# A hand-ordered attention + gated FFN kernel: TensorE's and ScalarE's steps of five periods in a new order, the other three engines' order kept

## The chip, the cores and the metric

The kernel runs on one core of a Trainium2 chip. The core has TensorE (PE, matrix products; loading a stationary operand is shown as PEld), VectorE (DVE), ScalarE (ACT), GpSimd (POOL) and SyncE (SP), each executing its own list of instructions in order, and 16 DMA engines that move data between the device memory and the on-chip memory. The metric is the device time of one execution in microseconds (us). The time of the kernel before is the median of 3 runs.

## The reference

Two stages follow each other. The first is attention of 64 heads (8 batches × 8 heads, 576 positions, 64 channels per head), in two forms that are added: a coarse one on queries, keys and values averaged over groups of 4 positions (144 by 144), whose result is repeated 4 times, and a local one in which position i sees only the positions j with |i − j| < 4. The second is a gated feed-forward layer on all 4608 positions.

```python
q_d = q.reshape(B, H, Sd, factor, D).mean(axis=3)      # and k_d, v_d; factor = 4
out_d = sm_attn(q_d, k_d, v_d)
out_up = np.repeat(out_d, factor, axis=2)
mask = np.abs(pos[:, None] - pos[None, :]) < factor
scores = np.where(mask, scale * np.matmul(q, k.transpose(0, 1, 3, 2)), -1e9)
out_local = np.matmul(softmax(scores), v)
attn_out = out_up + out_local                            # (8, 8, 576, 64)

x = attn_out.transpose(0, 2, 1, 3).reshape(4608, 512)
gate = np.maximum(x @ w_gate, 0.0)                       # w_gate, w_val: 512 x 1536
val = x @ w_val
return (gate * val) @ w_out                              # w_out: 1536 x 512
```

## The kernel before, in words

Inputs are float32 in memory and are made float16 on the way in; sums are float32 in PSUM, the accumulator memory of TensorE, which has 8 banks of 512 float32 columns.

**Tiling.** The 64 heads are taken as 32 pairs, four pairs to a batch. For the feed-forward layer the 4608 positions are cut into 9 chunks of 512 columns of `xT`, the transposed x. While one chunk goes through the feed-forward layer, the attention of later pairs is worked in between. What follows the start is therefore organised in periods: period c works on chunk c's gate and value products, on the output products of chunk c − 1, and on four head pairs further on (two in each half of the period; the half is the number u in a step's name, the pair of the half its letter a or b).

**The multiplication scheme.** The gate products (x times w_gate) from chunk 2 on and the output products are not done block by block but by a scheme of seven products instead of eight: the operands are cut in 2 × 2 blocks, sums and differences of blocks are formed ahead (VectorE), seven products are formed on TensorE, and the four result blocks come out of sums of products. Here this is class `Half7` (L1250 to L1274). Product 1 is accumulated in a quarter `a` of two PSUM banks; ScalarE copies it to quarter `d` (copy 1); products 6 and 7 are added to it, after copy 2 to quarter `b`, and so on. At the end ScalarE casts two of the result blocks (`finish` 11 and 21, L1270), and VectorE adds for the other two (`finish` 12 and 22, L1272) the saved product 5, which ScalarE had copied out (copy 5). Product 4 is added into the same quarter `a` in which product 7 ended, so TensorE may start it only after `finish` 22 has read that quarter, and `finish` 21 reads it after product 4. A quarter that is read late holds up the next product that goes there.

**The order.** Nothing is planned by a compiler here. A string `SEQ` (L18) holds 2,330 step names; the program runs through it (L1551) and issues each step's instructions to the engines concerned, in this order. Each engine then executes its own instructions in the order in which they were issued, and waits at an instruction until what it reads has been written and what it overwrites has been read. So the place of a name in the string matters only against other names that use the same engine.

**The names.** `kind/argument/u@c` is a step of half u of period c. Those that matter here:

- `sq/j.bank.tile.i`: product i of the gate scheme for blocks j (TensorE, L1254; two matmuls of 256 columns); `sk/….i`: its copy i (ScalarE, L1265); `sf/….11` and `.21`: ScalarE's casts (L1270); `sf/….12` and `.22`: VectorE's additions (L1272).
- `up`, `uk`, `uf`: the same for the output products of the chunk before (six matmuls each).
- `vh/jj.bank`: a value product (TensorE, L910; four matmuls of 512 columns); `gt`: VectorE multiplies it with the gate (L1349).
- `hg`, `hv`, `relu`, `gate`: chunk 1's gate and value products, in the plain way (L910, L919, L922).
- `scores`, `o/…`: attention's matmuls (L807, L811; L838, L853, L858); `exp` (ScalarE, L820) and `ed` (L825): its exponentials; `mask` (VectorE, L833); `ln`, `inv` (ScalarE), `xn`, `xsum` (VectorE): its normalisation.
- `kk/…` (ScalarE, L770): key columns copied into the block-diagonal form that the local scores use; `kd/…` (ScalarE, L777): the same for the pooled keys, after VectorE's pooling `pool` (L530); `zero/…`: one-time clearing.
- `next`, `sum`, `sumhi`, `xq` (VectorE, L989, L1241): operand sums of the seven-product schemes.
- `v1` (L575), `v2` (L567), `tm` (L1483), `tn` (L1424), and the loads `qk`, `v` (L462, L480): GpSimd; `v4`, and some of the transposes (`flip`): SyncE's queue.
- `t:…`: the steps of the last chunks, behind period 6 (L1158 and others).

In the string before, periods 2 to 6 repeat one and the same order. In period 5 (and in each of the others) ScalarE's part of the first half reads: `kk/b0 uk/2.1 sk/4.0.0.1 kk/b1 sf/4.0.0.11 sk/4.0.0.2 sk/4.0.0.5 exp/a0 ed/a kk/a1 sf/4.0.0.21 uk/2.2 uk/2.5 sk/0.0.2.5 …`, and TensorE's: `… sq/4.0.0.6 vh/4.7 sq/4.0.0.3 sq/4.0.0.7 up/2.5 sq/4.0.0.4 up/2.6 sq/0.0.2.1 …`.

Of the kernel before, what the change touches and what calls it, by code (L numbers as in the profile page):

```python
# [48 lines left out]
o/a00/0@1 o/a01/0@1 qk/a3/0@1 zs/1.0/0@1 tn/1/0@1 gate/0/0@1 c21//0@1 o/a10/0@1 ln/a/0@1 p/3/0@1 flip/11 next/3/0@1  # L49
qk/b3/0@1 c12//0@1 relu/2/0@1 qk/b1/0@1 o/a11/0@1 inv/a/0@1 pool/b/0@1 xn/a/0@1 hg/1/0@1 relu/1/0@1 zero/b/1 v2/a/1@1  # L50
hg/4/0@1 zero/b/5 hv/1/0@1 gate/1/0@1 hv/2/0@1 qk/b0/0@1 vd/9/7 vc/9/7 hg/3/0@1 relu/3/0@1 flip/12 gate/2/0@1
xsum/a/0@1 zs/2.0/0@1 scores/b/0@1 exp/b0/0@1 mask/b0/0@1 exp/b1/0@1 mask/b1/0@1 qk/a3/1@1 hv/3/0@1 gate/3/0@1 vd/10/2
ed/b/0@1 zs/3.0/0@1 vc/10/2 v4/b/1@0 hv/4/0@1 relu/4/0@1 gate/4/0@1 pool/a/0@1 tn/3/0@1 o/b00/0@1 o/b01/0@1 ln/b/0@1
v/b/1@0 o/b10/0@1 o/b11/0@1 p/1/1@1 inv/b/0@1 xn/b/0@1 hg/5/0@1 keep/1/1@1 hv/5/0@1 p/2/1@1 c11//1@1 p/6/1@1
scores/a/1@1 flip/13 relu/5/0@1 hg/0/1@1 qk/a0/1@1 zero/b/2 p/5/1@1 xsum/b/0@1 qk/a1/1@1 exp/a0/1@1 keep/2/1@1 p/7/1@1
mask/a0/1@1 gate/5/0@1 exp/a1/1@1 mask/a1/1@1 ed/a/1@1 o/a00/1@1 relu/0/1@1 pool/b/1@1 qk/a2/1@1 qk/b0/1@1 keep/3/1@1
c22//1@1 zero/d/0 v/a/0@1 pool/a/1@1 v2/b/0@1 v4/b/0@1 v1/a/1@1 o/a01/1@1 ln/a/1@1 o/a10/1@1 o/a11/1@1 v/b/0@2
# [12 lines left out]
up/2.7/0@2 sk/0.0.2.1/0@2 uf/2.22/0@2 sq/0.0.2.6/0@2 sk/0.0.2.2/0@2 ln/a0/0@2 inv/a/0@2 pool/b/0@2 next/0/0@2  # L70
up/2.2/0@2 o/a10/0@2 sq/0.0.2.3/0@2 sq/0.0.2.2/0@2 sf/0.0.2.11/0@2 sq/0.0.2.7/0@2 v1/a/0@2 after/3/0@2 sf/0.0.2.22/0@2
sf/0.0.2.12/0@2 kd/b0/0@2 o/a11/0@2 xn/a0/0@2 up/2.4/0@2 kd/b1/0@2 up/2.3/0@2 uf/2.21/0@2 v2/b/0@2 uf/2.11/0@2
uf/2.12/0@2 sq/0.0.2.4/0@2 sf/0.0.2.21/0@2 pool/a/0@2 sq/1.1.0.1/0@2 sq/1.1.0.5/0@2 sk/1.1.0.5/0@2 scores/b/0@2
v4/b/0@2 vh/0.7/0@2 sk/1.1.0.1/0@2 sq/1.1.0.6/0@2 v1/b/0@2 exp/b0/0@2 gt/0.7.2/0@2 vh/6.3/0@2 gt/6.3.3/0@2 mask/b0/0@2
sk/1.1.0.2/0@2 kd/a0/0@2 sq/1.1.0.2/0@2 sq/1.1.0.7/0@2 sf/1.1.0.22/0@2 ed/b/0@2 kd/a1/0@2 sq/1.1.0.3/0@2 kk/a0/0@2
v4/a/0@2 vh/1.0/0@2 o/b00/0@2 sf/1.1.0.11/0@2 kk/b1/1@2 sq/1.1.0.4/0@2 sf/1.1.0.21/0@2 o/b01/0@2 sf/1.1.0.12/0@2
ln/b0/0@2 o/b10/0@2 sq/2.2.0.1/1@2 sq/2.2.0.5/1@2 vh/7.1/0@2 o/b11/0@2 xsum/a/0@2 sk/2.2.0.1/1@2 next/2/0@2
sq/2.2.0.6/1@2 sq/2.2.0.2/1@2 inv/b/0@2 scores/a/1@2 sk/2.2.0.5/1@2 gt/1.0.0/0@2 qk/a1/1@2 gt/7.1.1/0@2 xn/b0/0@2
sk/2.2.0.2/1@2 v1/a/1@2 up/0.1/1@2 tm/b/0@2 qk/b3/1@2 sq/2.2.0.7/1@2 v/a/1@2 ed/a/1@2 sq/2.2.0.3/1@2 sf/2.2.0.11/1@2
kk/a0/1@2 up/0.5/1@2 sf/2.2.0.22/1@2 sq/2.2.0.4/1@2 sf/2.2.0.21/1@2 next/1/0@2 v2/b/1@2 uk/0.1/1@2 sf/2.2.0.12/1@2  # L80
qk/a0/1@2 qk/a2/1@2 vh/8.7/1@2 pool/b/1@2 qk/a1/0@3 sq/3.2.1.1/1@2 up/0.6/1@2 gt/8.7.1/1@2 exp/a0/1@2 mask/a0/1@2
# [24 lines left out]
gt/7.1.1/0@3 xn/b0/0@3 sk/2.2.0.2/1@3 v1/a/1@3 up/0.1/1@3 tm/b/0@3 qk/b3/1@3 sq/2.2.0.7/1@3 v/a/1@3 ed/a/1@3
sq/2.2.0.3/1@3 sf/2.2.0.11/1@3 kk/a0/1@3 up/0.5/1@3 sf/2.2.0.22/1@3 sq/2.2.0.4/1@3 sf/2.2.0.21/1@3 next/1/0@3 v2/b/1@3
# [1475 lines left out]
```

## Time and profile before

| | before |
|---|---|
| median of 3 runs | 342.25 us (341.89 to 342.35) |
| the profiled execution's own time | 342.53 us |
| its span, first to last instruction | 340.7 us |
| granted TensorE clock, mean | 1.000 |
| busy: PE, DVE, ACT, POOL | 332.2, 288.6, 269.0, 189.1 us |
| `SEQ` steps | 2,330 |

The page is one profiled execution. Busy times are sums over instructions; TensorE's matmuls overlap in its pipeline and their ends are modelled, so that a matmul is listed with 0.27 to 0.38 us though the next may start 0.11 or 0.22 us behind it. In the timeline a row gives start, duration, engine, line, operation, output and inputs, the shape, how many instructions of the kind are joined in it (xN), and in brackets how long the engine was idle before it and what ended that. In the table by stretch of time, each engine has its busy time and in brackets the instructions that it started.

### The profile page before, as it was taken

To read this page: it belongs to the slowest core of one execution; us is meant where nothing else is said; L and a number is where in the kernel's file an instruction comes from. 1 tells how busy PE (TensorE), PEld (TensorE's weight loads), DVE (VectorE), ACT (ScalarE), POOL (GpSimd) and SP (SyncE) were. 2 spreads that over 40 slices of the span, in tenths; PEclk is the share of its full clock that TensorE was granted. 3 is DMA by queue.
4 is the path that set the end of the run, shared out by engine and by line. 5 is a ranking of instruction groups with operands and counts; after the bars stand their busy time and mean duration, and the time that the engine had idled before them with its cause. 6 is when DMAs were issued, how large, how long until landed. Compare 5 with 4: busy or idle time off the path is not lost.

```text
span 340.7 us, 9149 instructions
## 1 busy us (share of the span) xinstructions
PE 332.2 (97%) x3458; PEld 243.5 (71%) x3458; DVE 288.6 (85%) x574; ACT 269.0 (79%) x649; POOL 189.1 (56%) x268
## 2 busy tenths in 40 slices
PE   8899999999999999999999999999999999999996
PEld 3665556656567786878677868787778768888875
DVE  6695679998799998989899989998998898897692
ACT  3877786788998988889888888988898647896842
POOL 8984655939978769848993997855610000000000
PEclk9999999999999999999999999999999999999999
DMA  9999999999999999999999999999300102003014
GB/s 136 166 170 208 185 194 168 136 215 130 179 162 170 183 79 228 141 187 95 229 102 165 134 175 160 197 106 194 55 31 2 64 0 95 1 17 108 3 56 131
DMA packets 162176, 43.92 MB, mean 129 GB/s; under 512 B 147500, under 2 KB 156820, under 8 KB 162132
## 3 DMA queue, kind: packets, MB, share of 16 engines
q0 software_dynamic: 123136, 19.51, 79.7%
q1 hardware_dynamic: 38884, 23.80, 31.7%
q8 instruction: 27, 0.44, 0.6%
q14 instruction: 17, 0.14, 0.1%
q10 hardware_dynamic: 112, 0.02, 0.0%
HBM read 46.59 MB, written 9.44 MB: 164 GB/s over the span
## 4 chain that ended last, share of the span: by engine, by line
PE 76%; DMA 8%; ACT 5%; POOL 4%; DVE 4%; issue 2%; SPq 0%; DVEq 0%; ACTq 0%; POOLq 0%
PE ps L1254 23%; PE ps L910 22%; PE ps L1158 17%; DMA qk<-in_k_dram 3%; DMA wv_sb<-in_moe_w_val_dram 3%; PE ps L995 3%; DMA qkT<-qk 2%; PE ps L838 2%; POOL qk L457 2%; PE ps L811 1%; PE ps L858 1%; PE ps L853 1%; POOL vw L507 1%; PE ps L807 1%; DVE xT L1134 1%
## 5 line engine op out<-in xcount | busy, mean ns | idle before, releaser
L910 PE MATMUL ps<-xT,wv_sb 128*128 128x512 f16 x352 | 89.3, 379 | 0.0
L910 PEld LDWEIGHTS <-wv_sb 128*128 128x128 f16 x352 | 32.4, 97 | 27.6
L1349 DVE SCALAR_TENSOR_TENSOR gT<-r,ps 128x512 f16<-128x512 f16 x55 | 37.4, 681 | 5.9 <-PE ps L910 5.1
L462 POOL DMA_DIRECT2D qk<-in_k_dram x46 | 33.5, 732 | 15.8 <-DMA qkT<-qk 12.7
L1254 PE MATMUL ps<-xT,qk 128*128 128x256 f16 x240 | 40.9, 272 | 0.0
L462 POOL DMA_DIRECT2D qk<-in_q_dram x46 | 34.0, 740 | 9.1 <-DMA qkT<-qk 4.4
L1265 ACT COPY ps<-ps 128x256 f32<-128x256 f32 x80 | 29.1, 368 | 7.5 <-PE ps L1254 6.9
L1254 PE MATMUL ps<-xT,wg_sb 128*128 128x256 f16 x180 | 33.8, 272 | 0.8 <-DVE xT L1272 0.4
L530 DVE TENSOR_REDUCE qkd<-qkT 128x288 f16<-128x1152 f16 x23 | 30.8, 1338 | 0.0
L480 POOL DMA_DIRECT2D vw<-in_v_dram x40 | 28.8, 729 | 2.0 <-DMA qk<-in_k_dram 1.1
L1270 ACT CAST r<-ps 128x256 f16<-128x256 f32 x55 | 20.2, 367 | 11.0 <-DVE r L1272 6.3
L1169 ACT COPY ps<-ps 128x256 f32<-128x256 f32 x54 | 19.4, 366 | 9.1 <-PE ps L1158 7.3
L575 POOL TENSOR_TENSOR vd<-v 48x192 f16<-48x192 f32 x40 | 25.6, 641 | 1.7
L910 PE MATMUL ps<-xT,wg_sb 128*128 128x512 f16 x104 | 26.1, 380 | 0.5 <-DMA wg_sb<-in_moe_w_gate_dram 0.3
L567 POOL TENSOR_TENSOR v<-v 112x384 f32<-112x384 f32 (+1 forms) x21 | 21.8, 1036 | 7.1 <-DMA v<-in_v_dram 6.5
L1254 PEld LDWEIGHTS <-qk 128*128 128x128 f16 x240 | 22.2, 97 | 4.8
L1254 PEld LDWEIGHTS <-xo 128*128 128x128 f16 x240 | 22.6, 97 | 2.9 <-DVE xo L989 0.2
L1254 PE MATMUL ps<-wt,xo 128*128 128x256 f16 x180 | 24.5, 272 | 0.0
L1254 PEld LDWEIGHTS <-wg_sb 128*128 128x128 f16 x180 | 17.0, 97 | 10.2 <-issue 2.7
L888 ACT ACTIVATE rden<-rden 128x720 f32<-128x720 f32 x28 | 22.5, 804 | 0.8
L922 DVE TENSOR_TENSOR gT<-r,ps 128x512 f16<-128x512 f16 x24 | 16.2, 681 | 7.0 <-PE ps L910 3.3
L1272 DVE TENSOR_TENSOR r<-ps,xT 128x256 f16<-128x256 f32 x44 | 18.0, 417 | 4.5 <-PE ps L1254 3.3
(175 smaller groups left out, 879.3 us busy)
## 6 DMA issues: line engine op xcount, KB each, us to landing
out_dram<-y_sb SPq DMA_DIRECT2D x24, 256.0 KB, 2.9
v<-in_v_dram SPq DMA_DIRECT2D x20, 192.0 KB, 5.0
qk<-in_k_dram POOLq DMA_DIRECT2D x46, 72.0 KB, 5.3
qk<-in_q_dram POOLq DMA_DIRECT2D x46, 72.0 KB, 5.1
vw<-in_v_dram POOLq DMA_DIRECT2D x38, 80.0 KB, 4.5
v<-in_v_dram SPq DMA_DIRECT2D x20, 144.0 KB, 5.0
out_dram<-y_sb SPq DMA_DIRECT2D x22, 128.0 KB, 1.8
vw<-in_v_dram POOLq DMA_DIRECT2D x12, 168.0 KB, 6.5
```

Source lines behind the costliest of these rows:

```text
L462: nc.gpsimd.dma_start(dst.rearrange("p (j h d) -> p j h d", h=2, d=64)[:, :, hh, :], _dap(src, off + hh * S * D, [[D, 96], [NQ * D, NB], [ ...
L480: nc.gpsimd.dma_start(t[lo : lo + 64, j0:j1, lo : lo + 64], _dap(v, base + j0 * QB * D, [[D, 64], [QB * D, j1 - j0], [1, D]]),)
L530: nc.vector.tensor_reduce(out=qkd[hp % 2].rearrange("p i t -> p (i t)"), in_=qkT[hp % 4][:, 0 : 2 * S].rearrange("p (t f) -> p t f", f=4), ...
L567: nc.gpsimd.tensor_tensor(out=m, in0=t[:, :, 0:128], in1=t[:, :, 128:256], op=ALU.add)
L575: nc.gpsimd.tensor_tensor(out=vp[hp % 3][lo : lo + 48, :, lo : lo + 64], in0=m[:, :, 0:64], in1=m[:, :, 64:128], op=ALU.add)
L888: nc.scalar.activation(out=rden, in_=rden, func=AF.Exp, scale=-1.0)
L910: nc.tensor.matmul(out=out, lhsT=w[:, kk, bass.ts(jj, 128)], rhs=xT[:, kk, c * TCH : (c + 1) * TCH], start=(kk == 0), stop=(kk == 3),)
L1158: nc.tensor.matmul(out=out, lhsT=self.left[i][t], rhs=self.right[i][t], start=(i == 1 and t == 0), stop=(t == n - 1), skip_group_check=True,)
L1254: nc.tensor.matmul(out=out, lhsT=self.left[i - 1][k], rhs=self.right[i - 1][k], start=(i == 1 and k == 0), stop=(k == n - 1), skip_group_c ...
L1265: nc.scalar.copy(out=o, in_=x)
L1270: nc.scalar.copy(out=o, in_=self.d if i == 11 else self.a)
L1349: lambda c, jj, b, t: nc.vector.scalar_tensor_tensor(out=gT[c % 2][:, jj, :], in0=tg[t], scalar=0.0, in1=ps[:, b, :], op0=ALU.max, op1=ALU ...
```

## The change

Only the string `SEQ` differs; the steps in it are the same 2,330, each as often as before. The new string has one line more, so the lines behind it are numbered one higher. The program that results has, on VectorE (574 instructions), GpSimd (268) and SyncE (119), the same instructions in the same order, but for which of four output buffers `y_sb` is meant in a few of them. On TensorE 941 of the 3,458 matmuls stand at another place, by at most 30 matmuls, and on ScalarE 280 of 650 instructions, by at most 16. The first step that moves is `o/a11/0@1` in chunk 1, the last are in the second half of period 6; what is ahead of and behind that is as it was. The five periods no longer have one common order; each has its own.

The core of the diff, for the beginning of period 5 (before, then after):

```diff
-kd/a1/1@4 qk/b1/0@5 up/2.1/0@5 xq/0/0@5 xq/1/0@5 kk/b0/0@5 sq/4.0.0.1/0@5 xq/2/0@5 scores/a/0@5 vh/10.6/0@5 uk/2.1/0@5
-sk/4.0.0.1/0@5 sq/4.0.0.2/0@5 sq/4.0.0.5/0@5 sq/4.0.0.6/0@5 sumhi/0/0@5 kk/b1/0@5 vh/4.7/0@5 sf/4.0.0.11/0@5 xq/3/0@5
-sk/4.0.0.2/0@5 v2/a/0@5 sq/4.0.0.3/0@5 next/0/1@4 sk/4.0.0.5/0@5 sq/4.0.0.7/0@5 up/2.5/0@5 sumhi/1/0@5 exp/a0/0@5
-ed/a/0@5 next/1/1@4 kk/a1/0@5 sf/4.0.0.22/0@5 sq/4.0.0.4/0@5 sf/4.0.0.21/0@5 mask/a0/0@5 sf/4.0.0.12/0@5 gt/4.7.0/0@5
...
+kd/a1/1@4 sq/4.0.0.1/0@5 xsum/b/1@4 up/2.1/0@5 gt/11.1.1/1@4 qk/b1/0@5 sk/4.0.0.1/0@5 uk/2.1/0@5 xq/0/0@5 xq/1/0@5
+xq/2/0@5 scores/a/0@5 sumhi/0/0@5 xq/3/0@5 v2/a/0@5 next/0/1@4 sumhi/1/0@5 next/1/1@4 vh/10.6/0@5 sq/4.0.0.5/0@5
+sq/4.0.0.6/0@5 exp/a0/0@5 sq/4.0.0.2/0@5 vh/4.7/0@5 sk/4.0.0.5/0@5 sk/4.0.0.2/0@5 sq/4.0.0.7/0@5 sf/4.0.0.11/0@5
+kk/b0/0@5 up/2.5/0@5 sq/4.0.0.3/0@5 kk/a1/0@5 sf/4.0.0.22/0@5 mask/a0/0@5 sq/4.0.0.4/0@5 up/2.6/0@5 sf/4.0.0.21/0@5
+ed/a/0@5 uk/2.2/0@5 sq/0.0.2.1/0@5 uk/2.5/0@5 sq/0.0.2.5/0@5 sf/4.0.0.12/0@5 gt/4.7.0/0@5 sum/2/0@5 o/a00/0@5
```

ScalarE's own order for the first half of three periods in the new string, so that the single moves can be followed:

```
period 2: kk/b1 kk/b0 sk/4.0.0.1 zero/b/3 uk/2.1 sf/4.0.0.11 sk/4.0.0.5 sk/4.0.0.2 exp/a0 ed/a sf/4.0.0.21 uk/2.2 uk/2.5
          sk/0.0.2.1 kk/a1 … sk/1.1.0.2 kd/a0 exp/b0 ed/b sf/1.1.0.11 kk/a0 kd/a1 sf/1.1.0.21
period 3: kk/b0 uk/2.1 sk/4.0.0.1 ed/a sf/4.0.0.11 sk/4.0.0.5 sk/4.0.0.2 exp/a0 kk/a1 sf/4.0.0.21 …
          ed/b sf/0.0.2.21 exp/b0 sk/1.1.0.2 kd/a1 sk/1.1.0.5 sf/1.1.0.11 kk/a0 kd/a0 sf/1.1.0.21
period 5: sk/4.0.0.1 uk/2.1 exp/a0 sk/4.0.0.5 sk/4.0.0.2 sf/4.0.0.11 kk/b0 kk/a1 sf/4.0.0.21 ed/a uk/2.2 uk/2.5 …
          uf/2.11 exp/b0 sk/1.1.0.1 sk/1.1.0.5 sk/1.1.0.2 ed/b sf/1.1.0.11 kk/b1/1 kd/a0 kd/a1 sf/1.1.0.21
```

and for the second half of period 2, before and after:

```
before: sk/2.2.0.1 inv/b sk/2.2.0.5 sk/2.2.0.2 ed/a sf/2.2.0.11 kk/a0 sf/2.2.0.21 uk/0.1 exp/a0 kd/b0 sk/3.2.1.1 sk/3.2.1.5
        uk/0.2 uk/0.5 sk/3.2.1.2 sf/3.2.1.11 kk/b0 kd/b1 ln/a0 …
after:  sk/2.2.0.1 sk/2.2.0.5 inv/b sk/2.2.0.2 sf/2.2.0.11 kk/b1 ed/a uk/0.1 exp/a0 sf/2.2.0.21 kk/a0 uk/0.2 sk/3.2.1.5
        sk/3.2.1.1 kk/b0 kd/b1 sk/3.2.1.2 sf/3.2.1.11 uk/0.5 kd/b0 ln/a0 …
```

More of the change, by code (lines that the diff above doesn't have):

```diff
@@ L53 @@
[L53 to L57, printed above, removed]
@@ new lines @@
+kk/a0/1@6 qk/b3/1@6 p/3/0@1 hg/1/0@1 hv/2/0@1 relu/2/0@1 flip/11 next/3/0@1 qk/b3/0@1 c12//0@1 qk/b1/0@1 pool/b/0@1
+ln/a/0@1 zero/b/5 inv/a/0@1 xn/a/0@1 relu/1/0@1 zero/b/1 hv/1/0@1 hg/4/0@1 v2/a/1@1 gate/1/0@1 qk/b0/0@1 flip/12
+gate/2/0@1 xsum/a/0@1 v/a/0@6 qk/a3/0@6 qk/b2/0@6 v4/a/0@6 v/a/1@6 vd/9/7 vc/9/7 hg/3/0@1 relu/3/0@1 scores/b/0@1
+hv/3/0@1 exp/b0/0@1 exp/b1/0@1 ed/b/0@1 relu/4/0@1 hv/4/0@1 vd/10/2 vc/10/2 qk/a1/1@6 zs/2.0/0@1 mask/b0/0@1
+mask/b1/0@1 o/b00/0@1 o/b11/0@1 o/b10/0@1 o/b01/0@1 p/1/1@1 hg/5/0@1 ln/b/0@1 inv/b/0@1 qk/a0/0@6 qk/a1/0@6 keep/1/1@1
```

380 lines of the change are left out of this document (190 added, 190 removed).

## The prediction

> **What bounds the kernel now.** I read the page first: busy shares, the 40 slices, the chain that ended last; then the busy time by stretch, the waits, and single waits in the timeline. All times are microseconds.
>
> ```profile
> PE 332.2 (97%) x3458; PEld 243.5 (71%) x3458; DVE 288.6 (85%) x574; ACT 269.0 (79%) x649; POOL 189.1 (56%) x268
> ...
> PE   8899999999999999999999999999999999999996
> ...
> DMA  9999999999999999999999999999300102003014
> ...
> PE 76%; DMA 8%; ACT 5%; POOL 4%; DVE 4%; issue 2%; SPq 0%; DVEq 0%; ACTq 0%; POOLq 0%
> ```
>
> TensorE is at work for 97% of the span, in every slice but the first two and the last, and most of the chain is its own. The DMA engines are full until about 247 (slice 29), so loads must be watched though they hardly appear in the chain.
>
> ```profile
> core 0: us, PE busy (x) PEld busy (x) DVE busy (x) ACT busy (x) POOL busy (x), PEclk, DMA share, GB/s
> 66.70:101.00 34.30, 34.05 (x354) 20.39 (x351) 29.25 (x54) 30.23 (x60) 26.18 (x38) 1.00 1.79 174
> 101.00:118.00 17.00, 16.95 (x175) 13.22 (x174) 16.14 (x28) 14.88 (x36) 13.74 (x21) 1.00 1.29 167
> 118.00:152.60 34.60, 34.09 (x337) 25.54 (x336) 31.96 (x58) 29.40 (x71) 25.91 (x40) 1.00 1.29 159
> 152.60:187.20 34.60, 34.54 (x343) 25.95 (x342) 32.08 (x58) 30.48 (x72) 27.35 (x39) 1.00 1.31 150
> 187.20:221.80 34.60, 34.60 (x347) 26.41 (x345) 31.51 (x58) 30.28 (x73) 30.44 (x45) 1.00 1.51 165
> 221.80:256.40 34.60, 34.49 (x346) 26.30 (x345) 31.81 (x58) 30.12 (x72) 15.86 (x24) 1.00 0.69 93
> ```
>
> These stretches cover the part in which orders differ: TensorE's first moved step is at 66.7, its last at 255.6. TensorE is never visibly idle long; VectorE has 2.5 to 3.1 free in a period of 34.6, ScalarE 4.1 to 5.2. So the change can win only TensorE's short starts delayed by an operand, and can lose as much as it likes, since the others have little slack. "Busy" hides most of those delays, because a matmul's modelled end runs on. I measured them by starts: back to back, matmuls start 0.109 apart at 256 columns (18 in 1.97 in the chain) and 0.216 at 512. A start later than that, with the awaited instruction ending at that moment, is a wait.
>
> ```profile
> 151.58 1.97 PE ps L1254 x18
> ...
> 88.66 0.81 PE L910 MATMUL ps<-xT,wg_sb 128*128 128x512 f16 x3 [0.18 <-ACT r L919]
> ...
> 253.69 0.38 PE L910 MATMUL ps<-xT,wv_sb 128*128 128x512 f16 x1
> ```
>
> The first and the last of 27 such waits, at 88.66 and 253.69, are shown. Together they cost 4.18: 16 on ScalarE (2.47), 11 on VectorE (1.72). That is the most the change can remove; 332.2 of 340.7 stays.
>
> **The change part by part.** Nothing is added or removed: the same 2,330 steps in another order. TensorE gets 941 of 3,458 matmuls elsewhere (by at most 30 matmuls), ScalarE 280 of its 650 instructions (by at most 16). VectorE's, GpSimd's and SyncE's queues keep their order, and with them every DMA issue; work per instruction is unchanged, so the sum is waits alone. Here is the commonest one, from period 5.
>
> ```profile
> 206.61 0.42 DVE L1272 TENSOR_TENSOR r<-ps,xT 128x256 f16<-128x256 f32 x1 [0.54 <-PE ps L1254]
> 206.95 0.72 ACT L770 COPY kk<-qkT 64x640 f16<-64x640 f16 x1
> 207.09 0.38 PE L1254 MATMUL ps<-xT,wg_sb 128*128 128x256 f16 x2
> 207.31 0.82 PE L1254 MATMUL ps<-wt,xo 128*128 128x256 f16 x6
> 207.69 0.37 ACT L1270 CAST r<-ps 128x256 f16<-128x256 f32 x1
> 208.12 0.38 PE L1254 MATMUL ps<-xT,wg_sb 128*128 128x256 f16 x2
> 208.12 0.10 PEld L1254 LDWEIGHTS <-wg_sb 128*128 128x128 f16 x1 [0.17 <-issue]
> ```
>
> (1) `sq/0.0.2.1` (208.12) waits for the cast `sf/4.0.0.21` (207.69, ends 208.06), which stands behind `kk/a1` (0.72), `ed` and `exp`. In the five periods it costs .22, .15, .16, .16, .28. In the new order `kk/a1` goes behind the cast in period 2, `ed` in 4, both in 6, and in 3 `ed` goes ahead of earlier copies: gone, 0.81. In period 5 `kk/b0` and `kk/a1` both stand directly ahead of it: 0.16 stays.
>
> (2) `sq/4.0.0.4` (207.09) waits for VectorE's `sf/4.0.0.22` (206.61, ends 207.03), which needs `sq/4.0.0.7`. The new order runs product 7 before product 3 in all five periods, so product 3's two matmuls (0.22) fill the wait: .17, .10, .09, .09, .08 gone, 0.53.
>
> (3) `vh/7.1` (253.69) waits for the cast `sf/1.1.0.21`, five times 0.11, because `kk/b1/1` (0.72) stands directly ahead of the cast.
>
> ```profile
> 253.27 0.37 ACT L1270 CAST r<-ps 128x256 f16<-128x256 f32 x1
> ...
> L770 ACT COPY kk<-qkT 64x640 f16<-64x640 f16 x20 | 14.5, 723 | 0.3
> L820 ACT ACTIVATE att<-ps 128x576 f16<-128x576 f32 x20 | 13.1, 655 | 0.0
> L825 ACT ACTIVATE att<-ps 128x432 f16<-128x432 f32 x20 | 10.6, 531 | 0.0
> L777 ACT COPY cst_sb<-qkd 64x144 f16<-64x144 f16 x40 | 12.3, 308 | 2.9 <-DVE qkd L530 2.5
> ```
>
> That copy moves to the second half in periods 2, 3, 4 and 6, and stays two to three places ahead in 5: 0.43 gone.
>
> (4) Chunk 1 and the entry to period 2, with waits at 88.66, 91.35, 99.00, 100.83 and 104.04 (.62): `hg/3` gets `hg/2` and `hv/1` between itself and `hg/1`, and `sk/4.0.0.1` goes ahead of `zero/b/3` and `uk/2.1`. I take 0.55.
>
> (5) In period 2 ScalarE itself stands still for VectorE's pooling, and TensorE pays .31 and .09 right behind.
>
> ```profile
> 120.33 0.31 ACT L777 COPY cst_sb<-qkd 64x144 f16<-64x144 f16 x1 [1.07 <-DVE qkd L530]
> 120.96 0.10 PEld L1254 LDWEIGHTS <-wg_sb 128*128 128x128 f16 x1 [0.43 <-issue]
> ```
>
> `kd/b0`, which waits there, stood right behind `exp/a0`; in the new order seven other copies come between `exp/a0` and the first `kd/b`: 0.40 gone. What is late next is the row of `sk`/`sf` copies itself, which then follows TensorE.
>
> (6) The largest single wait is not touched. GpSimd's value step starts just ahead of VectorE's `next` sum, which then takes 1.39 instead of 0.55; TensorE stands 0.53 behind it.
>
> ```profile
> 141.49 1.00 POOL L567 TENSOR_TENSOR v<-v 112x384 f32<-112x384 f32 x1
> 141.51 1.39 DVE L989 TENSOR_TENSOR xo<-gT 128x768 f16<-128x768 f16 x1
> 143.29 0.20 PEld L1254 LDWEIGHTS <-wg_sb 128*128 128x128 f16 x2 [0.53 <-issue]
> ...
> L989 DVE TENSOR_TENSOR xo<-gT x24: 216/550/1391, 99.6 to 253.5; 128x768 f16<-128x768 f16 x15, 128x640 f16<-128x640 f16 x5, 128x128 f16<-128x128 f16 x4
> ```
>
> Five waits of this kind (143.29 to 178.63) cost 1.13. Both queues keep their order, so I leave them at nothing gained.
>
> Removed: .81 + .53 + .43 + .55 + .40 = 2.72.
>
> New tight places in the order: period 5, `kk/b0` and `kk/a1` ahead of `sf/4.0.0.21`; period 2, `uk/0.5` behind `kk/b0`, `kd/b1` and two `sk`/`sf` copies (it frees the output's correction `uf/0.22`); `exp/b0` ahead of the first `sk/1.1.0` copies in 3, 4 and 5; period 2, `kk/b1/1` between the casts `sf/2.2.0.11` and `.21`. Six places. Upper bound: TensorE pays the whole operation each time, .72 + (.72 + .31) + 3 × .655 + .72 = 4.4. Lower bound 0: TensorE has other matmuls between. The nearest rows are (1) and (3), where a 0.72 copy directly ahead of a cast cost .11 to .28. I take about .17 each, 1.0. A gain by fewer changes of matmul shape I put at nothing.
>
> Loads and tail. An earlier TensorE meets the same loads: `vd` was made at 213.35 (212.76 + 0.59), 4.4 before TensorE took it, so 2 off does not reach them.
>
> ```profile
> 212.76 0.59 POOL L575 TENSOR_TENSOR vd<-v 48x192 f16<-48x192 f32 x1
> ...
> 217.72 0.35 PE L838 MATMUL ps<-att,vd 128*128 128x144 f16 x3
> ...
> 267.81 0.69 DVE L1349 SCALAR_TENSOR_TENSOR gT<-r,ps 128x512 f16<-128x512 f16 x1 [0.60 <-PE ps L910]
> ...
> 276.56 0.10 PEld L1158 LDWEIGHTS <-vw 128*128 128x128 f16 x1 [0.89 <-DVE vw L989]
> ```
>
> The tail's one real wait (276.56) is for VectorE, whose work there waited for TensorE at 267.81; so the tail, unchanged in order, moves as a whole with TensorE.
>
> Sum: −2.72 + 1.0 = −1.7. Span 340.7 to 339.0. The profiled execution took 342.53, 0.28 above the median of three runs, 342.25; it goes to 340.8, the median to 340.5. The granted clock is 1.00 in every stretch above, so no term is one of the clock.
>
> **The rivals.**
> R1, the new places are free and half of (6) vanishes, because VectorE's and GpSimd's relative time shifts: −2.72 − .57 = −3.3, 339.0. For it: most new places have 4 to 8 matmuls between. Against it: the collisions need only a shift of 1.
>
> R2, the order does what it says, but the gain does not arrive: VectorE, with 2.5 to 3.1 free per period and its order fixed, becomes the pace, or waits for loads move with it. 342.2. For it: 31.5 to 32.1 busy of 34.6, and GpSimd, whose orders feed VectorE and the loads, stands long.
>
> ```profile
> POOL seen L1483 <- DVE att L833: 14.0, 7, 4.1
> ...
> POOL qk L462 <- DMA qkT<-qk: 10.7, 4, 3.5
> ```
>
> Against it: these are waits with slack behind them, and no wait of TensorE is for a load here.
>
> R3, slower. VectorE's and GpSimd's orders are kept, their moments are not: TensorE's new order shifts when VectorE gets its operands. Seven of the 24 `next`/`sum` rows are slow now, the first and the last of them these (the first row holds a slow one of 1.2 and a normal one of 0.22):
>
> ```profile
> 100.05 1.42 DVE L989 TENSOR_TENSOR xo<-xo,gT 128x128 f16<-128x128 f16 x2
> ...
> 222.44 0.97 DVE L989 TENSOR_TENSOR xo<-xo,gT 128x768 f16<-128x768 f16 x1
> ```
>
> Most are 768 wide and cost VectorE up to 1.391 − .550 = 0.84. If four more meet `v2` (1.00) and TensorE, which now has less distance, pays in full: 4 × .84 = 3.4, so −1.7 + 3.4 = +1.7, 343.9. It decides from two such delays on (no gain), from three on (2.5) it is slower. Against it: TensorE paid 1.1 of the seven's 4.4 or so, a quarter.
>
> The Trainium skill, "SBUF — State Buffer", section "Who interferes with whom", has VectorE and GpSimd share one port pair as an exclusive lock, so that the loser is fully blocked. By that rule the row at 141.51 would be 1.00 + 0.55 − 0.02 = 1.53; it was 1.39, so the trace roughly agrees, and every collision would cost VectorE nearly the whole 1.00 rather than 0.84.
>
> **How the numbers follow.** Forecast 0.52 (340.5), R1 0.17 (339.0), R2 0.13 (342.2), R3 0.18 (343.9). Range 338.8 to 343.5: it leaves out about half of R3's upper part and the edge of R1; new places at 4.4 instead of 1.0 would give 343.9, at 0 give 339.5. The forecast's own range, without other signs, is 339.5 to 341.5. A difference counts from 0.2%, 0.68. Faster (under 341.57): .52 + .17 less .03 of the forecast's edge, 0.66. Same: R2 and that edge, 0.16. Slower: R3, 0.18.
>
> **What would show it.** Right: in the changed trace the waits ahead of `sq/0.0.2.1` and `sq/4.0.0.4` are gone in four and five periods; the 1.07 of ScalarE on L530 is gone; 0.53-like waits behind slow L989 stay; the tail from `t:` on has the same length; VectorE's busy time stays at 288.6. Step (1) is wrong if another copy is late in its place. The prediction is wrong if L989's slow rows number well over seven, if TensorE shows a wait over 0.5 for ScalarE at one of the six places, or if loads appear ahead of TensorE.

## The result, and the profile after

| | before | after |
|---|---|---|
| median (lowest to highest, 6 runs each) | 342.23 us (341.89 to 342.46) | 340.44 us (340.07 to 341.04) |
| ratio | | 0.9942, 95% interval 0.9916 to 0.9968 |
| profiled execution: span | 340.7 us | 338.9 us |
| granted clock | 1.000 | 0.999 |
| TensorE's waits between 66.7 and 255.7 us, measured as in the prediction | 27, 4.18 us | 15, 2.51 us |
| span less these waits | 336.5 us | 336.4 us |

The change gained 1.79 us; 340.5 had been forecast. The waits fell by 1.67, the span by 1.8. The page of the profile after, with the lines that answer to those shown of before:

```profile
PE 330.7 (98%) x3458; PEld 243.4 (72%) x3458; DVE 290.0 (86%) x574; ACT 268.9 (79%) x649; POOL 189.7 (56%) x268
...
PE 79%; DVE 6%; DMA 6%; POOL 4%; issue 2%; ACT 1%; DVEq 0%; POOLq 0%
```

In the chain that ended last ScalarE's share went from 5% to 1% and VectorE's from 4% to 6%: the change cured waits for ScalarE (2.47 us before, 0.74 after) and left those for VectorE (1.72 and 1.77). The stretches of time, as before (busy us of each engine with the instructions started; clock, DMA share and GB/s at the end):

```profile
66.70:101.00 34.30, 33.76 (x352) 20.07 (x347) 30.07 (x53) 29.95 (x60) 27.24 (x39) 1.00 1.78 173
101.00:118.00 17.00, 17.00 (x176) 13.54 (x177) 16.47 (x30) 14.01 (x35) 12.77 (x19) 1.00 1.35 162
118.00:152.60 34.60, 34.60 (x348) 26.48 (x346) 31.70 (x60) 31.20 (x74) 27.77 (x42) 1.00 1.44 167
...
221.80:256.40 34.60, 34.48 (x346) 26.27 (x345) 32.50 (x60) 29.20 (x72) 15.61 (x24) 1.00 0.62 87
```

The gain lies in the middle: from 118.0 to 152.6 TensorE started 348 matmuls instead of 337. In the first stretch it started 352 instead of 354; nothing was won there. Matmuls differ in width, so this count is rough; VectorE's instructions, whose order is the same in both, start at the same time as before at 102.5, 1.5 us earlier at 152.6, and 1.8 earlier from 263 on. Of the waits that the trace itself puts down to TensorE's queue, the largest group was, in the stretch 66 to 256 of the kernel before (engine, line, what it waited for: us in total, times, longest)

```profile
PEld L1254 <- issue: 2.7, 10, 0.5
```

and in the same stretch after

```profile
PEld L1255 <- issue: 1.1, 6, 0.3
...
PEld L808 <- ACT cst_sb L778: 0.8, 3, 0.3
PEld L1255 <- DVE xo L990: 0.6, 1, 0.6
```

A period after, in the timeline (start, duration, engine, line, operation; in brackets the idle time ahead of it and what ended that):

```profile
135.66 0.42 DVE L1273 TENSOR_TENSOR r<-ps,xT 128x256 f16<-128x256 f32 x1 [0.22 <-PE ps L1255]
135.72 0.72 ACT L771 COPY kk<-qkT 64x640 f16<-64x640 f16 x1
...
136.27 0.38 PE L1255 MATMUL ps<-xT,wg_sb 128*128 128x256 f16 x2
...
136.69 0.37 ACT L1271 CAST r<-ps 128x256 f16<-128x256 f32 x1 [0.24 <-PE ps L1255]
```

This is `sf/4.0.0.22`, `kk/a1`, `sq/4.0.0.4` and `sf/4.0.0.21` of period 3, the place of steps 1 and 2. VectorE's addition ends at 136.08, 0.19 before product 4 starts; and the cast now waits for TensorE (0.24), not TensorE for the cast, though `kk/a1` still stands directly ahead of it.

### The profile page after: what moved, and what is told of

Read it like the earlier page. It is cut to its first block, busy times and chain, and to the rows that moved or that the text cites. A ratio compares the mean times of both kernels' runs of the same rounds, so it can differ in the third digit from the quotient of the medians.

```text
span 338.9 us, 9143 instructions
## 1 busy us (share of the span) xinstructions
PE 330.7 (98%) x3458; PEld 243.4 (72%) x3458; DVE 290.0 (86%) x574; ACT 268.9 (79%) x649; POOL 189.7 (56%) x268
## 4 chain that ended last, share of the span: by engine, by line
PE 79%; DVE 6%; DMA 6%; POOL 4%; issue 2%; ACT 1%; DVEq 0%; POOLq 0%
PE ps L1255 24%; PE ps L911 24%; PE ps L1159 17%; DMA qk<-in_k_dram 3%; DMA wv_sb<-in_moe_w_val_dram 3%; PE ps L996 3%; PE ps L839 2%; POOL qk L458 2%; PE ps L854 1%; PE ps L812 1%; PE ps L859 1%; DVE xo L990 1%; POOL vw L508 1%; DVE gT L1350 1%; PE ps L808 1%
## 5 line engine op out<-in xcount | busy, mean ns | idle before, releaser
L481 POOL DMA_DIRECT2D vw<-in_v_dram x40 | 29.7, 771 | 2.4 <-DMA qk<-in_q_dram 1.4
L1484 POOL COPY seen<-att 112x1 f16<-112x1 f16 x16 | 6.1, 383 | 24.8 <-DVE att L834 24.5
```

The costliest lines, as they stand in the source:

```text
L481: nc.gpsimd.dma_start(t[lo : lo + 64, j0:j1, lo : lo + 64], _dap(v, base + j0 * QB * D, [[D, 64], [QB * D, j1 - j0], [1, D]]),)
```

## The experiments

Ratios are to the kernel before, measured on the same chip beside each; e1 to e4 ran on one chip, e5 to e8 on a second, e9 to e12 on a third. "Waits" are TensorE's between 66.7 and 255.7 us in the profiled execution.

| kernel | median us | ratio (95%) | span | waits | span less waits |
|---|---|---|---|---|---|
| after, again (e11) | 340.62 | 0.9930 (0.9905–0.9956) | 337.3 | 7, 1.53 | 335.8 |
| e1 TensorE's order alone | 367.79 | 1.0733 (1.0701–1.0766) | 365.2 | 47, 22.56 | 342.6 |
| e2 ScalarE's order alone | 358.79 | 1.0462 (1.0426–1.0499) | 358.7 | 39, 20.17 | 338.5 |
| e7 as e1, bank pairs kept | 353.73 | 1.0322 (1.0284–1.0360) | 350.9 | 49, 15.24 | 335.7 |
| e8 as e2, bank pairs kept | 354.11 | 1.0320 (1.0278–1.0363) | 352.1 | 42, 15.24 | 336.9 |
| e3 three moves | 344.90 | 1.0062 (1.0038–1.0086) | 343.7 | 37, 7.25 | 336.5 |
| e6 moves into idle slots | 341.33 | 0.9962 (0.9940–0.9985) | 339.4 | 19, 2.62 | 336.8 |
| e4 before, three v2 paced | 342.16 | 0.9988 (0.9968–1.0009) | 341.7 | 31, 5.07 | 336.6 |
| e5 after, v2 paced | 339.57 | 0.9899 (0.9868–0.9929) | 338.1 | 7, 1.61 | 336.5 |
| e12 the same again | 339.26 | 0.9903 (0.9877–0.9928) | 337.0 | 4, 0.79 | 336.2 |
| e9 moves and v2 paced | 340.32 | 0.9938 (0.9912–0.9964) | 338.2 | 13, 1.68 | 336.5 |
| e10 after without step 2 | 342.47 | 0.9976 (0.9946–1.0006) | 340.7 | 22, 4.48 | 336.2 |

The last column carries the reading of all of them: but for e1 and e2 it lies between 335.7 and 336.9, over waits from 0.8 to 15.2. A kernel of this family takes some 336 us of span and TensorE's waits on top. In the traces of e1 and e2 the granted clock was lower, 0.986 and 0.995 against 0.999 to 1.000 in all others; as an estimate that is 0.014 × 365.2 = 5.1 and 0.005 × 358.7 = 1.8 us, most of the 6 and 2 us by which these two stand above the rest. A profiled execution is one draw, so its span need not stand where the median does (after: 338.9 and 337.3).

**e1 and e2: one engine's new order alone.** The string of e1 gives TensorE its new sequence and the other four engines their old one; e2 gives ScalarE the new one. In period 3, for instance:

```diff
 TensorE in e1, period 3
-sq/4.0.0.6 vh/4.7 sq/4.0.0.3 sq/4.0.0.7 up/2.5 sq/4.0.0.4
+sq/4.0.0.6 vh/4.7 sq/4.0.0.7 sq/4.0.0.3 up/2.5 sq/4.0.0.4
 ScalarE in e2, period 3
-sk/4.0.0.1 kk/b1 sf/4.0.0.11 sk/4.0.0.2 sk/4.0.0.5 exp/a0 ed/a kk/a1 sf/4.0.0.21
+sk/4.0.0.1 ed/a sf/4.0.0.11 sk/4.0.0.5 sk/4.0.0.2 exp/a0 kk/a1 sf/4.0.0.21
```

> TensorE in the new order, ScalarE and the other three in the old one. Separable theory (each step of the prediction is worth its wait by itself): steps 2 and 4 go with TensorE, 0.53 and some 0.5, steps 1, 3 and 5 stay, because ScalarE's copies stand where they stood; TensorE's waits fall from 4.2 to about 3.2 and the time from 342.2 to 341.2 to 341.7. Rival (the two orders only work as a pair): TensorE now reaches products before ScalarE's old order has served them, so new waits outweigh those removed and the time is 343 or more.

> ScalarE in the new order, TensorE and the other three in the old one. Separable theory: steps 1, 3 and 5 go with ScalarE (0.81 + 0.43 + 0.40), steps 2 and 4 stay; TensorE's waits fall from 4.2 to about 2.6 to 3.0 and the time from 342.2 to 340.7 to 341.2. Rival (the two orders only work as a pair): ScalarE now waits for products that TensorE's old order brings later, and the time is 342.2 or more.

Measured: 25 us and 16 us slower. The theory by which each step of the prediction is worth its wait by itself fell at once, and the rival of both expectations (the two orders only work as a pair) held. But a part of this came from how the two orders were merged. In e1's timeline (VectorE, then ScalarE)

```profile
164.01 0.41 DVE L1273 TENSOR_TENSOR r<-ps,xT 128x256 f16<-128x256 f32 x1
```

```profile
164.46 0.37 ACT L1271 CAST r<-ps 128x256 f16<-128x256 f32 x1 [3.41 <-DVE r L1273]
```

ScalarE's cast `sf/3.2.1.11` stands still for 3.41 us until VectorE's `sf/3.2.1.12` is done, though each only reads, from different columns of the same PSUM bank. So a name's place in the string counts not only against names of its own engine, as the description of the kernel had it: two steps of different engines in one PSUM bank also wait for each other in the string's order. (The cast and the addition also write into one tile, `r`, in different columns, so these rows alone don't tell the bank from the tile. Copy 5 in e3 below does: in period 6 it writes a tile that product 7 doesn't touch, and waits 0.66 for it, at 243.00, as in the other periods.) (The Trainium skill, "PSUM — Partial Sum Buffer", section "PSUM bank collisions raise a hardware error", says that two engines must not be in one bank of the same partitions at once and that accesses are to be guarded by bank. No run here shows the error; the wait in the rows above is what the guard costs.)

**e7 and e8: the same, with the bank pairs kept.** Edit: the two merges again, with every pair of steps in one PSUM bank in the direction that both strings have; of the pairs in which they differ, those of ScalarE and VectorE as in ScalarE's string.

> TensorE in the new order, ScalarE in the old one, as in the first such run, but each pair of steps of two engines in the same PSUM bank is issued in the order that both strings share, or in the old one where they differ between ScalarE and VectorE. If the 25 us of the first run came from pairs that the merging turned round (such as the cast sf/3.2.1.11 waiting 3.4 for VectorE's sf/3.2.1.12), the time falls to 341 to 343. If TensorE's and ScalarE's orders need each other, it stays above 346.

> ScalarE in the new order, TensorE in the old one, with the pairs in one PSUM bank issued as both strings have them, or as the new one has where they differ between ScalarE and VectorE. If turned pairs made the 16 us of the first such run, the time falls to 341 to 343. If the two orders need each other, it stays above 346.

Measured: 1.0322 and 1.0320, 11 us slower each, the second case of both expectations. Without the turned pairs 14 of e1's 25 us and 5 of e2's 16 are gone; what stays is the mismatch of the two orders itself. Of the 14, as an estimate, 3 to 5 are the clock, which was 0.986 to 0.991 in e1's runs and 1.000 in e7's. In e7's waits from 66 to 256

```profile
PEld L1255 <- issue: 9.8, 26, 0.7
```

and in e8's timeline, ScalarE's copy 2 and product 2 behind it, `sq/2.2.0.2`:

```profile
230.23 0.38 ACT L1266 COPY ps<-ps 128x256 f32<-128x256 f32 x1
230.66 0.38 PE L1255 MATMUL ps<-xT,wg_sb 128*128 128x256 f16 x2 [0.73 <-ACT ps L1266]
```

The waits are many and middling, mostly for ScalarE (10.2 of 15.2 us in e7, 11.7 in e8). Each half of the change alone costs 11 us; both together gain 1.8. Neither engine's order brings any of the gain by itself.

**e3: the three moves as the prediction reasoned them.** In the old order, in each of periods 2 to 6 (`kk/b1` of the second half went behind that half's `ed/a`):

```diff
-sk/4.0.0.2/0@3 v2/a/0@3 sq/4.0.0.3/0@3 next/0/1@2 sk/4.0.0.5/0@3 sq/4.0.0.7/0@3 up/2.5/0@3
+sk/4.0.0.2/0@3 v2/a/0@3 sq/4.0.0.7/0@3 sq/4.0.0.3/0@3 next/0/1@2 sk/4.0.0.5/0@3 up/2.5/0@3
...
-kk/a1/0@3 sf/4.0.0.22/0@3 sq/4.0.0.4/0@3 sf/4.0.0.21/0@3 ... up/2.6/0@3 uk/2.2/0@3 uk/2.5/0@3
+sf/4.0.0.22/0@3 sq/4.0.0.4/0@3 sf/4.0.0.21/0@3 ... up/2.6/0@3 uk/2.2/0@3 uk/2.5/0@3 kk/a1/0@3
```

> The old order with three kinds of steps moved in each of periods 2 to 6: kk/a1 behind uk/2.5, kk/b1 of the second half behind ed/a of the second half, product 7 of sq/4.0.0 ahead of its product 3. If the waits named in steps 1, 2 and 3 are caused by what stands ahead of the awaited step, all 15 of them go (0.97 + 0.53 + 0.54 = 2.0) and the time is 340.2 to 340.6. If ScalarE is simply late there by its load, the wait moves to the next copy and the time is 341.5 to 342.2.

Measured: 0.6% slower, past the worse of the two cases; waits 7.25. The ten waits for the two casts are gone, as reasoned, and others came. Two mechanisms, both in period 5 of its timeline:

```profile
206.83 0.36 ACT L1265 COPY ps<-ps 128x256 f32<-128x256 f32 x1
207.84 0.37 ACT L1265 COPY xT<-ps 128x256 f32<-128x256 f32 x1 [0.66 <-PE ps L1254]
...
210.47 0.72 ACT L770 COPY kk<-qkT 64x640 f16<-64x640 f16 x1
...
211.49 0.38 ACT L1265 COPY ps<-ps 128x256 f32<-128x256 f32 x1
...
211.92 0.38 PE L1254 MATMUL ps<-xT,qk 128*128 128x256 f16 x2 [0.24 <-ACT ps L1265]
```

Copy 5 (207.84) now waits 0.66 for product 7, which came ahead of it in the string and lies in the same bank; ScalarE loses that in four of the five periods, and `sq/4.0.0.4`'s wait grew from 0.09 to 0.21 instead of going. And `kk/a1` (210.47) only handed its 0.72 to the next row of copies: `sq/0.0.2.6` (211.92) waits 0.41 for copy 1, more than the 0.16 saved at `sq/0.0.2.1`. Another 1.9 of the 7.25 lie at 104 to 109 behind two slow sums of VectorE (1.36 and 1.71, usually 0.55); whether these belong to the edit or to this execution, one trace doesn't show.

**e6: the same moves into places where ScalarE was idle.** In the old trace ScalarE stands still 0.86 to 0.91 behind `sk/0.0.2.1`; behind the second half's `exp/a0` it is 1.07, 0.25, 0.26, 0.68 and 0.26 in periods 2 to 6. The two copies went there, and copy 5 went ahead of product 7:

```diff
-sk/4.0.0.2/0@3 v2/a/0@3 sq/4.0.0.3/0@3 next/0/1@2 sk/4.0.0.5/0@3 sq/4.0.0.7/0@3 up/2.5/0@3
+sk/4.0.0.2/0@3 sk/4.0.0.5/0@3 v2/a/0@3 sq/4.0.0.7/0@3 sq/4.0.0.3/0@3 next/0/1@2 up/2.5/0@3
...
-o/a00/0@3 o/a01/0@3 up/2.7/0@3 sk/0.0.2.1/0@3 uf/2.22/0@3 sq/0.0.2.6/0@3 sk/0.0.2.2/0@3
+o/a00/0@3 o/a01/0@3 up/2.7/0@3 sk/0.0.2.1/0@3 kk/a1/0@3 uf/2.22/0@3 sq/0.0.2.6/0@3 sk/0.0.2.2/0@3
```

> The old order with the three kinds of moves again, but each copy put where ScalarE stood still in the old trace (kk/a1 behind sk/0.0.2.1, where it had 0.86 idle; kk/b1 of the second half behind exp/a0, 0.68 idle), and with copy 5 of sq/4.0.0 issued ahead of product 7, so that it doesn't wait for that product in the same PSUM bank. If a moved copy costs nothing only in an idle slot, the 15 waits (2.0) go, nothing new of more than 0.1 per period comes, and the time is 340.2 to 340.8. If any local move sets off the rest of the period, new waits of 1 us or more appear and the time is 342 or more, as with the three moves before.

Measured: 0.9962 (0.9940 to 0.9985), between the two cases. All 15 waits are gone. What came instead is small: `sq/4.0.0.7` now waits for copy 5, 0.09 in periods 3 to 5 and 0.31 and 0.20 in 2 and 6, and `sq/3.2.1.6` 0.087 in four periods. Fifteen steps moved on their engines bring half to two thirds of what the new order brings (0.38% against 0.58%, or 0.70% in e11; the intervals overlap), where the same fifteen in e3, a few places off, cost 0.6%. That the idle slots make this difference is argued, not shown: e3 and e6 differ in the places of both copies and in copy 5 at once, and the second copy (0.72) is longer than the idle time at its new place in four of the five periods.

**e4: VectorE's slow sums, in the old order.** `tn` is a one-column copy on GpSimd that waits for the sum it reads:

```diff
-uf/2.21/0@3 v2/b/0@3 uf/2.11/0@3
+uf/2.21/0@3 tn/0/0@3 v2/b/0@3 uf/2.11/0@3
```

The same went ahead of `v2/a` (which moved behind `sum/3`) and `v2/b` of period 4.

> The old order; GpSimd's v2 step in periods 3 (once) and 4 (twice) waits, by a one-column copy put ahead of it, until VectorE's next or sum step beside it is done. If the overlap with v2 makes the sums slow and TensorE's five waits at 143 to 179 us come from that (step 6), the three sums take 0.55 instead of 1.39, 1.35 and 0.62, the five waits (1.13) go, and the time is 341.0 to 341.3. If the sums are slow for another reason, they stay slow and the time is 342.2; if the later v2 makes TensorE's next value products late, it is above 342.5.

Measured: no difference that can be told (0.9968 to 1.0009), though the five waits and two of the three sums behaved as step 6 said: the sum of period 3 took 0.55 (it had been 1.39), the first of period 4 as well (1.35), while the second of period 4, paced too, kept its 0.61. Behind the first, GpSimd's step ran beside operations that take one operand from PSUM, at no cost to them:

```profile
142.42 0.55 DVE L989 TENSOR_TENSOR xo<-gT 128x768 f16<-128x768 f16 x1
...
143.10 0.19 POOL L1486 COPY seen<-xo 128x1 f16<-128x1 f16 x1 [0.64 <-DVE xo L989]
...
143.24 1.00 POOL L567 TENSOR_TENSOR v<-v 112x384 f32<-112x384 f32 x1
143.55 0.90 DVE L873 TENSOR_TENSOR xn<-ps,rden 128x720 f16<-128x720 f32 x1
```

All five waits are gone, but others came elsewhere, some of them at 104 to 109 us, before the first edit:

```profile
104.19 1.21 POOL L567 TENSOR_TENSOR v<-v 112x384 f32<-112x384 f32 x1
104.47 1.35 DVE L989 TENSOR_TENSOR xo<-gT,xo 128x768 f16<-128x768 f16 x1
...
240.50 1.03 POOL L567 TENSOR_TENSOR v<-v 112x384 f32<-112x384 f32 x1 [3.42 <-DMA v<-in_v_dram]
240.59 1.84 DVE L989 TENSOR_TENSOR xo<-xo,gT 128x128 f16<-128x128 f16 x2
```

The row at 240.50 shows one reason: GpSimd's step starts when a load has landed (here after 3.42 us of waiting), and that moment need not be the same in every execution; e11 looks at this.

**e11: the new order once more.**

> The new order itself once more, to stand beside the others on one chip: 340.1 to 341.0, and its slow sums, if they depend on the moment at which loads arrive, at other places than in its first trace.

Measured: 340.62. In its first trace the new order has ten slow steps of VectorE between 66 and 256 (5.8 us longer than usual in all), in its second five (3.1). The same place in both, first

```profile
99.47 1.09 POOL L568 TENSOR_TENSOR v<-v 112x384 f32<-112x384 f32 x1
...
99.63 1.29 DVE L990 TENSOR_TENSOR xo<-gT 128x640 f16<-128x640 f16 x1
...
100.97 0.39 PE L1255 MATMUL ps<-wt,xo 128*128 128x256 f16 x2 [0.35 <-DVE xo L990]
```

and then

```profile
98.59 0.48 DVE L990 TENSOR_TENSOR xo<-gT 128x640 f16<-128x640 f16 x1
...
99.43 0.82 PE L1255 MATMUL ps<-wt,xo 128*128 128x256 f16 x6
```

The step of GpSimd that starts at 99.47 in the first trace starts at 101.68 in the second; ahead of it GpSimd had waited 1.39 us for loads in the one and 2.62 in the other. So most of the collisions belong to the execution. Not all do: two sums are slow in both traces, 1.35 at 172.13 and 170.92, and 1.25 and 1.52 at 220.39 and 218.92, and both were slow in the kernel before (1.35 at 173.83, 0.97 at 222.44).

**e5 and e12: all of them paced, in the new order.** Ahead of `v2/a`, `v2/b` of every period's first half and `v2/b` of its second, and of two steps of chunk 1, a one-column copy that waits for the sum beside it (17 added; one, `tq`, reads another column). Where a v2 stood ahead of its sum in the string it moved behind it, one of them together with four loads and a `v4` of SyncE; GpSimd's and SyncE's orders stay as they were:

```diff
+sum/3/0@3 tn/3/1@2 v2/a/0@3 ... tn/0/0@3 v2/b/0@3 ... next/1/0@3 tn/1/0@3 v2/b/1@3
+next/1/1@1 tq/1/1@1 v2/b/1@1
```

> The new order; each of GpSimd's v2 steps from chunk 1 on that runs beside VectorE's next and sum steps waits, by a one-column copy ahead of it, until the sum beside it is done. In the trace of the new order eight of TensorE's waits (1.8 us) are for VectorE and most lie behind a slow sum. If those come from the overlap, the slow sums fall from ten to three or fewer and the time from 340.4 to 339.0 to 339.6. If an overlap only moves to other instructions of VectorE when the v2 steps move (as it did in part when three of them were paced in the old order), the slow rows stay about as many and the time is 340.0 to 341.5; if the later v2 or the loads behind it become late for TensorE, it is above 341.5.

> The new order with the paced v2 steps once more, beside the new order on one chip. If pacing is worth what TensorE's waits say (2.5 against 1.6 us), it is 0.6 to 1.2 us below the new order; if the difference was one of the runs, the two are equal within 0.3.

Measured: 339.57 and 339.26, ratios 0.9899 and 0.9903: the fastest kernel of this study. On one chip it is 1.36 us below the new order (339.26 against 340.62), more than the 0.6 to 1.2 expected; by the means of the runs it is 1.0, and the intervals of the two ratios overlap. Its six runs lie closer there, 338.75 to 339.83 against 338.30 to 341.65 in ten, but those of e5 span 2.0 us and the new order's first six only 1.0. The sums of the two forms in which e12 paces most, in the new order (min/median/max in ns)

```profile
L990 DVE TENSOR_TENSOR xo<-xo,gT x16: 210/486/1350, 66.1 to 255.3; 128x768 f16<-128x768 f16 x6, 128x128 f16<-128x128 f16 x5, 128x640 f16<-128x640 f16 x5
L990 DVE TENSOR_TENSOR xo<-gT,xo x10: 545/552/1354, 68.0 to 241.9; 128x768 f16<-128x768 f16 x10
```

and in e12

```profile
L991 DVE TENSOR_TENSOR xo<-xo,gT x16: 216/482/553, 65.7 to 253.2; 128x768 f16<-128x768 f16 x6, 128x128 f16<-128x128 f16 x5, 128x640 f16<-128x640 f16 x5
L991 DVE TENSOR_TENSOR xo<-gT,xo x10: 549/551/557, 67.6 to 239.7; 128x768 f16<-128x768 f16 x10
```

The slow ones are gone from these. The expectation that slow steps would fall to three or fewer failed all the same: e5 has ten, e12 seven, now on `mask`, `xsum` and other sums, beside GpSimd's other steps and beside the later v2 itself (in e5 `mask` took 1.22 and another sum 1.35 beside it); they cost VectorE 4.4 and 2.2 us, and TensorE waited 1.37 and 0.51 for VectorE in all.

**e9: moves and pacing in the old order.** e6's string with `tn` ahead of the same v2 steps of periods 2 to 6.

> The old order with the moves into idle slots and, beside them, GpSimd's v2 steps of periods 2 to 6 paced by the sum beside them. In all seven traces so far the span is 336 to 337 us and TensorE's waits between 66.7 and 255.7 us on top. If both edits keep what they brought alone, the waits fall from 2.6 to 1.5 to 2.0 and the time is 338.8 to 340.3, as low as the new order gets with the same pacing: then the new order as a whole is not needed for its gain. If the slots were idle only because of the moments at which GpSimd's steps fell, new waits come and the time is above 341.

Measured: 340.32, at the upper end of the first case; waits 1.68, of which 0.05 is for VectorE. It is level with the new order without pacing and 1.1 above the new order with it. So the new order is not needed for a gain of this size, but it is still worth something that the fifteen moves are not; some 0.5 of e9's waits are those of step 4 in chunk 1 and at the entry to period 2, which the moves leave alone.

**e10: one part of the new order undone.** `sq/4.0.0.3` ahead of `sq/4.0.0.7` again, in five periods:

```diff
-sq/4.0.0.7/0@3 ... sq/4.0.0.3/0@3 ... sq/4.0.0.4/0@3
+sq/4.0.0.3/0@3 sq/4.0.0.7/0@3 ... sq/4.0.0.4/0@3
```

> The new order with one part undone: product 3 of sq/4.0.0 goes ahead of product 7 again in all five periods. If step 2 of the prediction holds within the new order, sq/4.0.0.4 waits again for VectorE's addition, about 0.1 in each period, 0.5 in all, and the time rises from 340.4 to 340.9. If the rest of the new order has made room for the addition, no wait comes back and the time is 340.4. If the order around it depends on this pair, the waits rise by more than 1 and the time is above 341.5.

Measured: 342.47 (339.46 to 344.08), the third of the cases expected, 1.85 above the new order on the same chip, and the ratio's interval just includes the kernel before. The wait of step 2 comes back as the prediction had sized it, .096, .096, .096, .097 and .083, 0.47 in all:

```profile
136.44 0.42 DVE L1273 TENSOR_TENSOR r<-ps,xT 128x256 f16<-128x256 f32 x1 [0.44 <-PE ps L1255]
...
136.91 0.38 PE L1255 MATMUL ps<-xT,wg_sb 128*128 128x256 f16 x2
```

Behind it `sq/0.0.2.1` of period 5 waits 0.68 instead of 0.15, and TensorE's waits for VectorE are 3.26 in this trace, step 2's 0.47 among them (1.77 and 1.14 in the new order's two). That the rest follow from the edit and not from the execution isn't shown by one trace; the median says that something of the kind does.

## Why the prediction was right, and where its steps were not

*The bound and the sum.* That the change can move only TensorE's waits, and that the rest of the span stays, held to within 1 us in every run but e1 and e2 (336 us and waits), where the clock was lower too. Forecast was 4.18 − 2.72 + 1.0 = 2.46 of waits; 2.51 came, in the profiled execution. One place stands twice in this sum: the 0.16 that stays of step 1 in period 5 is in the 1.46 left over, and once more, with 0.17, among the six new places. (And its DMA row is full for 28 slices, to 238.5 us, not to 247; nothing in the sum hangs on that.)

*Steps 1 to 5, the waits removed.* Step 1: all gone but period 5's, 0.154 left where 0.16 was said. Step 2: gone but in period 6, where 0.289 stands behind a sum of 1.30. Step 3: all five gone, 0.54 for 0.43. Step 4: 0.04 left, where 0.07 was said. Step 5: gone, and VectorE's pooling holds ScalarE up by 0.2 in the stretch 100 to 256. The removed waits were foreseen to 0.2 us.

*The new tight places, 1.0.* Mis-sized, and at the wrong places. Of the six only the one in period 5 shows, with 0.154. ScalarE's other new waits are elsewhere: 0.27 at `scores/b` of periods 2 and 4 for `kd`, and 0.28 in the second half of period 4. All waits for ScalarE are 0.74 in the new order; by the prediction's sum some 1.3 would have stayed.

*Step 6, "nothing gained".* This step failed in what it said, by treating five waits as fixed places. The five were gone in the first trace after, though VectorE's and GpSimd's orders are the same. Of the three slow sums behind them only the first, at 141.51, was at its usual 0.55 in both traces after; the other two stayed slow (1.35 and 0.62, in e11 1.35 and 0.61), but TensorE now waits 0.22 behind them, at 177.8, instead of 0.49. Others came, at 71.7, 101.0 and 240.1 among them, and TensorE's waits for VectorE were 1.77 in one execution and 1.14 in the other, against 1.2 forecast (1.72 less 0.53). The error here and the one on the tight places, each about half a microsecond, went opposite ways; the forecast is closer than its parts. That they cancelled is luck.

*The reason given for steps 1 to 3.* The prediction put each wait down to the copy directly ahead of the awaited step. e3 shows that curing the wait in this way doesn't gain its time: putting that copy a few places on makes the kernel slower, and in the new order `kk/a1` still stands directly ahead of its cast in period 3 without harm. What matters is that the other engine's order fits (e7, e8) and, as e6 suggests, whether ScalarE has room where the step is put. The prediction priced the given pair of orders and was right for it; as prices of the moves by themselves its numbers are wrong, and where e1 to e3 were expected by them, they failed.

*The tail.* It moved as a whole: from product 5 of `up/0.5` in period 6 to the end, 84.0 us in both profiles (256.7 to 340.7, 254.9 to 338.9).

*The rivals.* R1's value, 339.0, is about what pacing added later. R2 did not happen: VectorE is busy for 32.5 of the last period's 34.6 us, and the gain still arrived. R3's mechanism was there, VectorE lost 5.8 instead of 4.2 us to slow steps in the first trace, but TensorE paid under a third of it. The prediction's "seven of the 24" takes its 24 from one of three forms; there are some 50 such sums. Slow by more than 0.1 us were seven of them before, nine in the first trace after and four in e11, so its sign of being wrong, "well over seven", did not come. The rule of the Trainium skill, "SBUF — State Buffer", section "Who interferes with whom" (a VectorE instruction with two inputs in on-chip memory contends with a GpSimd instruction that reads there), agrees with the rows of e4 above and with e12, where VectorE's pooling, one operand, keeps its 1.34 beside a full GpSimd step:

```profile
219.56 0.99 POOL L569 TENSOR_TENSOR v<-v 112x384 f32<-112x384 f32 x1
219.78 1.34 DVE L532 TENSOR_REDUCE qkd<-qkT 128x288 f16<-128x1152 f16 x1
```

## What to carry to other kernels

When one engine is busy for 97% of the span, list its late starts with what ended each: their sum bounds what an order can win, and here the span was that sum and a constant, within 1 us, while the sum ranged from 0.8 to 15.2 us (at a clock of 0.999 to 1.000). Price a given pair of orders by it, but don't price single moves by what stands ahead of a wait: look for room on its engine where the moved step goes, and for the pairs in one PSUM bank whose direction the move turns. Before polishing an order further, look for collisions that depend on when a load lands; 17 one-column copies that keep GpSimd's v2 steps out of VectorE's two-operand sums brought about half as much again as the whole reordering had (1.0 to 1.4 us on the chip where the reordering brought 2.2), though three such copies in the old order (e4) brought nothing that can be told.

## What the runs showed of the hardware that was not expected

Two traces of one and the same kernel differ by 1 us in TensorE's waits (2.51 and 1.53), with ten and five slow steps of VectorE, at a granted clock of 0.999 to 1.000. And some sums are slow although GpSimd's recorded step starts only after them, as here in the new order:

```profile
186.00 1.35 DVE L990 TENSOR_TENSOR xo<-xo,gT 128x768 f16<-128x768 f16 x1
187.13 1.07 POOL L568 TENSOR_TENSOR v<-v 112x384 f32<-112x384 f32 x1
```

The sum took 0.8 longer than usual and had 0.22 left when the other began by the record. With that step paced (e5 and e12) the sum is at its usual 0.55, but it is so in e11 without pacing too. So the cause stays open; whether GpSimd's recorded start is late, or its loads' issue ahead of it (two of 0.73 each) takes part, was not tried apart.

The granted clock fell three times where TensorE had stood still. In all fourteen traces it is idle for more than 1.5 us, between 66 and 256, only in e1 (3.09 us, until 166.6, and 3.05, until 249.0) and in e2 (2.40, until 85.6). Within 1.5 us of each restart the granted clock was 0.50 for some 3.4 us, and matmuls started twice as far apart (in e1 0.213 instead of 0.109 at 256 columns, in e2 0.427 instead of 0.216 at 512). On e1's page these are the second and third 8 of the clock's row (the first lies at 9 to 18 us, ahead of the change):

```profile
PEclk9899999999999999998999999998999999999999
```

So a long stop of TensorE cost more than its own length here; at half the clock for 3.4 us it is, as an estimate, 1.7 us each time. Why the clock fell no run shows.
